# mLSTM cell and SwiGLU block on one core: the first group rebuilt, weight halves on two queues

## The chip, the core and the metric

The kernel runs on one core of a Trainium2 chip. The core has five engines with queues of their own: TensorE (PE in the profile, with its weight loads shown as PEld), VectorE (DVE, V in the code), ScalarE (ACT, A), GpSimd (POOL, G) and SyncE (SP), which here only asks for DMAs. Each engine executes its instructions in the order in which the code emits them and waits on semaphores for the others. The metric is the time of one execution on the device in microseconds; the value of a kernel is the median of its runs.

## What is computed

The first part is an mLSTM cell over q, k, v of shape (4, 8, 768, 40) with input, forget and output gates. The second part is a feed-forward block on its output, 3072 tokens of 320 features.

```python
def _attn_ref(q, k, v, i_gate, f_gate, o_gate):
    for t in range(S):
        m_new = np.maximum(f_gate[:, :, t] + m, i_gate[:, :, t])
        f_stab = np.exp(f_gate[:, :, t] + m - m_new)
        i_stab = np.exp(i_gate[:, :, t] - m_new)
        C = f_stab * C + i_stab * np.einsum('bhd,bhe->bhde', vt, kt)
        n = f_stab * n + i_stab * kt
        h_tilde = np.einsum('bhde,bhe->bhd', C, qt)
        denom = np.maximum(np.abs(nq), 1.0)
        y[:, :, t] = sigmoid(o_gate) * h_tilde / denom
...
x = y.transpose(0, 2, 1, 3).reshape(3072, 320)
g = x @ w_gate
out = (g * sigmoid(g) * (x @ w_val)) @ w_out
```

The three weight matrices are float64 in memory; q, k, v and the gates are float32.

## The kernel before

**Groups.** The 768 positions are cut into six groups of 128 (`NG`). A group holds 128 tokens of each of the four batches, so 512 tokens go through the feed-forward block together. Partitions hold the 128 positions; the free dimension holds the 32 pairs of batch and head (`BH`), split into two halves `P` of 16. Group 0 has a path of its own (the functions `first_*`), because there is no earlier state. The later groups work on blocks of 64 positions.

**Group 0.** `load` (L137) brings k, q, v into tiles whose rows are 64, 64 and 41 words per head, of which 40 are filled from memory. `first_mask`, `first_inputs`, `first_maxima` (L530 to L542) add up the exponent of the decay weights of four heads in one PSUM bank by matmuls; eight banks, keyed (u, j) with batch u and half j of its heads. `first_exp(P)` takes the exponential on ACT into `W0`. `first_turn(P, ...)` (L556) transposes k or q of two heads at a time, 128 positions wide, into `kT`, `qT`. `first_scores(P)` (L565) forms the scores in four banks and V multiplies them into `W0` (L575). `first_own(u)` (L579) multiplies `W0` with v for one batch (`first_y`), `first_x(u)` divides, `first_gate(P)` applies the output gate, `first_seam(P, ...)` (L610) transposes x into `xT`, the right-hand side of the feed-forward block. `first_values` and `first_state` make the state for the next group. `burn` issues matmuls on zeros whose result nobody reads.

**Weights.** The hidden dimension 1536 is cut into 12 blocks of 128. A block's tile has the gate half of the weights on partitions 0 to 63 and the value half on 64 to 127. `piece_load(p)` (L161) asks for piece p: pieces 0 and 1 hold one block, the next five hold two, the last three hold a third of `w_out` each. A piece is three DMAs: the gate half on SP's queue, the value half as a large and a small one, on ACT's queue for p < 5, else on SP's. The words land in a raw buffer (two of a pool in turn, or a `home`, a tile that is free at that time). `convert(j)` makes float32 of the float64 words of a block in three steps: `scale` (two ACT operations, L212 and L214), `join` (two V operations, L221 and L222) and `rounded` (an addition on V or POOL, L229).

**The hidden layer of group 0.** `hidden(0, m)` (L698) makes block m: 20 matmuls into two banks `gv_ps` (L706; with four banks of that tag, PE can run one block ahead), then `first`, a list of conversions, then SiLU on ACT (L711) and the product on V (L712). The dictionary `ahead` says which conversions stand in block m, `slots` what is emitted behind block m: the loads, decay terms, turns, weights and scores of group 1. `project_all` (L719) follows with `o_ps`, and its dictionary `after` holds more of group 1 and the loads of group 2 (`early_squares` loads k of group 2 as 32 x 32 squares). Groups 1 to 5 run `gated` (L854) and `project_seven` (L777).

**Turns and seams of 64 rows.** `turn_one` (L313) and `seam` (L468), used for group 1, work on blocks of 64 positions with two banks each.

**Order.** Everything is in the order in which it is written (`manual_schedule`): an instruction that waits holds up all that stand behind it on its engine, and a DMA request waits on the queue of the engine that issues it.

The order in which the loads are asked for:

```python
for P in range(2):
    load(k_sb, k, 0, P)
    load(q_sb, q, 0, P)
    load(v_sb, v, 0, P)
load(o_sb, o_gate, 0, 0)
```

Of the kernel before, what the change touches and what calls it, by code (L numbers as in the profile page):

```python
# [12 lines left out]
U32 = mybir.dt.uint32  # L13
# [5 lines left out]
L = 128  # L19
# [5 lines left out]
def kernel(  # L25
# [128 lines left out]
    nc.scalar.dma_start(out=flat(f_sb), in_=gate_rows(f_gate)[:, L:])  # L154
    nc.scalar.dma_start(out=flat(i_sb), in_=gate_rows(i_gate)[:, L:])
# [3 lines left out]
    PIECES = [("gv", 0, 1), ("gv", 1, 1)] + [("gv", m, 2) for m in range(2, NFC, 2)] + [("o", m, 4) for m in range(0, NFC, 4)]  # L159

    def piece_load(p, home=None):  # L161
        kind, m, n = PIECES[p]
        if kind == "gv":
# [4 lines left out]
            queues = (nc.sync,) + 2 * (nc.scalar if p < 5 else nc.sync,)  # L168
        else:
            a, d = n, DM  # L170
            src = [(slice(0, 128), slice(0, n), moe_w_out[m * 128:(m + n) * 128].rearrange("(a p) d -> p a d", p=128))]
            queues = (nc.sync,)
        if src[0][2].dtype == F32:
            for r, cs, w in src:
# [6 lines left out]
        if home is None:  # L181
            raw = conv.tile([128, 4 * NKC * 128], U32, name="raw")
        else:
            raw = home.rearrange("p a t -> p (a t)").bitcast(U32)
        raw = raw[:, 0:2 * a * d]
        for (r, cs, w), queue in zip(src, queues):
            queue.dma_start(out=raw[r].rearrange("p (a d) -> p a d", a=a)[:, cs], in_=w.bitcast(U32))
# [47 lines left out]

    for P in range(2):
        load(k_sb, k, 0, P)
        load(q_sb, q, 0, P)
        load(v_sb, v, 0, P)
    load(o_sb, o_gate, 0, 0)  # L240
# [25 lines left out]
    idb = ident[0:BH, 0:BH]  # L266
    hot = early.tile([128, H], F32)
    cold = early.tile([128, H], F32)
    for u in range(B):
        r = slice(u * BH, (u + 1) * BH)  # L270
        nc.vector.tensor_copy(hot[r], ident[r, u * BH + u * H:u * BH + (u + 1) * H])
# [23 lines left out]
    def late_sums():  # L295
        nc.vector.tensor_tensor_scan(flat(f_sb), flat(keep1), flat(f_sb), 0.0, op0=ALU.mult, op1=ALU.add)
        nc.gpsimd.memset(step1, 0.0)
        nc.gpsimd.tensor_sub(i_sb, i_sb, f_sb)
# [191 lines left out]
    def weights_mask(P):  # L490
        for i in range(2):
            w = w_sb[half(i), heads(P)]
            nc.gpsimd.affine_select(w, w, compare_op=ALU.is_ge, fill=NEG, base=0, pattern=[[0, UH], [1, SUB]],  # L493
                                    channel_multiplier=-1)

# [26 lines left out]

    def rows(u):
        return slice(u * BH, (u + 1) * BH)
# [5 lines left out]
    def first_mask(u, j):  # L530
        wps[u, j] = bank("wps", "cell" if u < 2 else "gen").rearrange("p (h t) -> p h t", t=L)
        nc.tensor.matmul(wps[u, j], lhsT=ident_b, rhs=mask_b.unsqueeze(1).to_broadcast([128, HH, L]),
                         start=True, stop=False, skip_group_check=True)

    def first_inputs(u, j):
# [572 lines left out]
```

## Time and profile before

| what | value |
|---|---|
| median of 3 runs | 512.6 us (512.21 to 513.2) |
| the profiled execution | 513.3 us, its span 511.5 us |
| instructions | 14788 |
| PE busy | 505.1 us (99%) |
| DVE busy | 332.3 us (65%) |
| POOL busy | 255.0 us (50%) |
| ACT busy | 204.8 us (40%) |
| DMA | 43.27 MB in 205497 packets, mean 85 GB/s; 193432 packets are under 512 B |

The span runs from the first to the last instruction of the profiled execution, and that execution's own time is 1.8 us longer. A line of the timeline gives start, duration, engine, source line, operation, the tiles written and read, and how many instructions it merges; in brackets stands the idle time before it and what ended it. Matmuls overlap in the array, so a busy PE is not PE at its peak. A line of a window table gives the stretch, its length, then busy time (and count) of PE, PEld, DVE, ACT and POOL, the clock that PE was granted, the share of the DMA engines and their GB/s.

### The profile page before, as it was taken

What the parts mean: (1) busy time and instruction counts of PE and PEld (TensorE: products, weight loads), DVE (VectorE), ACT (ScalarE), POOL (GpSimd) and SP (SyncE); (2) the same over time, 40 slices, a digit from 0 to 9 for tenths busy, and PEclk for the clock granted to TensorE, in tenths of its full rate; (3) what the DMA queues carried; (4) which work ended last, traced back from release to release, by engine and by line L of the source; (5) the groups of instructions that cost most, each with busy time, mean ns of one, the idle gap of its engine ahead of it and who ended that gap; (6) DMA issues with size and microseconds to landing.
All of it is one profiled execution on the core that took longest, in us unless ns stands there. A gap on an engine that the chain in (4) does not pass through costs nothing.

```text
span 511.5 us, 14788 instructions
## 1 busy us (share of the span) xinstructions
PE 505.1 (99%) x6307; PEld 428.8 (84%) x6309; DVE 332.3 (65%) x539; ACT 204.8 (40%) x394; POOL 255.0 (50%) x274
## 2 busy tenths in 40 slices
PE   8999999999999999999999999999999999999997
PEld 4964445667888899988899888899988899988896
DVE  5779767887897777687466678467658554233421
ACT  3477655448512339312339321338421340223210
POOL 1303427475879663367652457652447650166710
PEclk9999999999999999999999999999999999999999
DMA  9999999698502992501993411993101200000001
GB/s 123 174 232 238 168 194 244 148 177 119 88 1 45 143 130 39 92 3 26 156 134 42 75 21 27 156 131 43 42 3 19 37 3 27 27 1 0 1 14 38
DMA packets 205497, 43.27 MB, mean 85 GB/s; under 512 B 193432, under 2 KB 200600, under 8 KB 205432
## 3 DMA queue, kind: packets, MB, share of 16 engines
q1 hardware_dynamic: 203444, 39.49, 49.4%
q10 hardware_dynamic: 1988, 2.85, 2.4%
q8 instruction: 49, 0.80, 0.7%
q14 instruction: 16, 0.13, 0.1%
HBM read 35.68 MB, written 4.01 MB: 78 GB/s over the span
## 4 chain that ended last, share of the span: by engine, by line
PE 91%; DMA 2%; DVE 2%; issue 1%; POOL 1%; ACT 1%; SPq 0%; DVEq 0%; ACTq 0%; POOLq 0%
PE gv_x L854 26%; PE o_ps L777 23%; PE gv_y L854 21%; PE gv_ps L706 5%; PE o_ps L723 5%; DMA w_sb<-M_dram 2%; PE inter L402 2%; PE intra L411 2%; PE sp L353 2%; PE first_y L582 1%; PE add L379 1%; POOL w_sb L493 1%; PE burn L521 1%; PE tp_kq L561 1%; PE sp L571 1%
## 5 line engine op out<-in xcount | busy, mean ns | idle before, releaser
L854 PE MATMUL gv_x<-xT,wgv_sb 64*128 64x256 f32 x720 | 89.1, 377 | 0.0
L854 PEld LDWEIGHTS gv_x<-xT,wgv_sb 64*128 64x128 f32 x720 | 69.6, 187 | 7.9 <-issue 0.2
L777 PE MATMUL o_ps<-wo_sb,h_sb 128*128 128x160 f32 x480 | 67.4, 300 | 0.0
L777 PEld LDWEIGHTS o_ps<-wo_sb,h_sb 128*128 128x128 f32 x480 | 65.6, 190 | 1.7 <-issue 1.7
L902 ACT ACTIVATE h_sb<-gv_x 128x256 f32<-128x256 f32 x30 | 11.5, 383 | 117.8 <-PE gv_x L854 117.8
L706 PE MATMUL gv_ps<-xT,wgv_sb 64*128 64x512 f32 x240 | 53.7, 596 | 0.3 <-DVE wgv_sb L229 0.3
L706 PEld LDWEIGHTS gv_ps<-xT,wgv_sb 64*128 64x128 f32 x240 | 23.6, 187 | 24.4 <-issue 23.2
L854 PE MATMUL gv_y<-q_sb,wgv_sb 64*128 64x256 f32 x360 | 44.0, 377 | 0.0
L854 PE MATMUL gv_y<-xT,wgv_sb 64*128 64x256 f32 x360 | 43.9, 376 | 0.0
L854 PEld LDWEIGHTS gv_y<-q_sb,wgv_sb 64*128 64x128 f32 x360 | 34.9, 187 | 4.2 <-DVE tmp L894 0.4
L854 PEld LDWEIGHTS gv_y<-xT,wgv_sb 64*128 64x128 f32 x360 | 35.0, 187 | 3.9
L364 POOL TENSOR_TENSOR vw_sb<-v_sb,w_sb 128x656 f32<-128x656 f32 x10 | 14.6, 1467 | 41.2 <-ACT w_sb L509 40.0
L777 PE MATMUL o_ps<-wT,S 128*128 128x160 f32 x240 | 33.4, 299 | 0.0
L777 PEld LDWEIGHTS o_ps<-wT,S 128*128 128x128 f32 x240 | 32.9, 190 | 0.0
L509 ACT ACTIVATE w_sb<-w_sb,g_T 128x64 f32<-128x64 f32 x128 | 31.0, 334 | 0.0
L854 PE MATMUL gv_x<-q_sb,sw 64*128 64x256 f32 x240 | 31.0, 376 | 0.0
L875 POOL TENSOR_TENSOR h_sb<-x_sb 128x512 f32<-128x512 f32 x12 | 15.8, 1314 | 24.6 <-ACT x_sb L874 24.6
L895 POOL TENSOR_TENSOR tmp<-tmp 128x512 f32<-128x512 f32 x15 | 20.0, 1332 | 14.5 <-DVE tmp L894 14.5
L875 POOL TENSOR_TENSOR h_sb<-tmp 128x512 f32<-128x512 f32 x13 | 16.5, 1269 | 21.5 <-ACT tmp L874 21.5
L744 POOL TENSOR_TENSOR S<-h_sb 128x256 f32<-128x256 f32 x30 | 22.6, 752 | 9.2 <-DVE h_sb L875 7.3
L854 PE MATMUL gv_y<-q_sb,sw 64*128 64x256 f32 x200 | 27.0, 388 | 0.0
L723 PE MATMUL o_ps<-wo_sb,h_sb 128*128 128x320 f32 x96 | 26.9, 437 | 0.0
(221 smaller groups left out, 984.6 us busy)
## 6 DMA issues: line engine op xcount, KB each, us to landing
w_sb<-M_dram SPq DMA_DIRECT2D x10, 512.0 KB, 7.1
k_sb<-in_k_dram SPq DMA_DIRECT2D x12, 320.0 KB, 7.4
v_sb<-in_v_dram SPq DMA_DIRECT2D x12, 320.0 KB, 5.5
o_sb<-in_o_gate_dram SPq DMA_DIRECT2D x12, 320.0 KB, 6.8
raw<-in_moe_w_out_dram SPq DMA_DIRECT2D x3, 1280.0 KB, 7.5
x_sq<-k_sb SPq DMA_DIRECT2D x64, 40.0 KB, 2.0
q_sb<-in_q_dram SPq DMA_DIRECT2D x32, 64.0 KB, 3.8
out_dram<-tmp SPq DMA_DIRECT2D x24, 80.0 KB, 1.7
```

Of the source, the lines that this page charges most:

```text
L353: nc.tensor.matmul(sp[two][half(i), a, :], lhsT=kT[feats(two), P * UA + a, half(i)], rhs=qT[feats(two), P * UA + a, half(i)], start=True, ...
L364: eng.tensor_tensor(vw_sb[:, heads(P)], v_sb[:, heads(P)], w_sb[:, heads(P), last].to_broadcast([128, UH, D1]), op=ALU.mult)
L402: nc.tensor.matmul(inter[two][half(i), a, :], lhsT=qT[feats(two), P * UA + a, half(i)], rhs=state(2 * n + i)[feats(two), P * UA + a, :], s ...
L509: nc.scalar.activation(w_sb[:, h], w_sb[:, h], AF.Exp, bias=g_T[:, n, h:h + 1], scale=-1.0)
L706: nc.tensor.matmul(ps[i], lhsT=wgv_sb[half(i), m, kc, :], rhs=x[half(i), kc, :], start=(kc == 0), stop=(kc == NKC - 1))
L723: nc.tensor.matmul(ps[u], lhsT=hid(g, m)[:, ts(u, L)], rhs=wo_sb[:, m, :], start=(m == 0), stop=(m == NFC - 1))
L744: eng.tensor_tensor(S1[:, k], lo[:, second_half], hi[:, second_half], op=ALU.add)
L777: nc.tensor.matmul(node[x][:, i], lhsT=lhs(k)[:, ts(i, L)], rhs=rhs(k), start=start and k == 0 and i == 0, stop=stop and k == KH - 1, skip ...
L854: nc.tensor.matmul(ps[:, i, cols], lhsT=lhs(c)[half(i)], rhs=rhs(c)[half(i)], start=start and c == 0, stop=stop and c == n - 1, skip_group ...
L875: (nc.vector if k == KH - 1 else nc.gpsimd).tensor_tensor(h_sb[:, 2 * k + 1], uw[:, 0], uw[:, 1], op=ALU.mult)
L895: nc.gpsimd.tensor_tensor(uw[:, :, second_half], uw[:, :, second_half], uw[:, :, first_half], op=ALU.add)
L902: nc.scalar.activation(h[:, first_half], x[:, 0, first_half], AF.Silu)
```

## The change

In group 0: q and k are loaded into a dense tile (part of `h_sb`) in the order q0, k0, q1, k1, then v; V and POOL spread them into the padded tiles. The exponent's banks are keyed (P, x), half P of the pairs and batch x, so that the first half's four banks are done before the second's begin. The turns and seams are those of 64 rows. `first_own` writes its output in two halves of 64 rows. Of the burns only the first stays; a `fill` of 14 matmuls stands before the hidden layer. Gating of the first half goes to POOL.

Weights: the first six blocks are six pieces of one block; all gate halves are asked for by SP, all value halves by GpSimd, and ACT asks for none. The rest of the gates f and i (positions 128 on) are asked for by SP after the first three gate halves. Conversions and group 1's preparation are spread anew over the slots; group 1's causal mask is a V maximum with a table (`weights_cap`) in place of POOL selections. In group 2's loads the k squares go ahead of o, and in group 1 the two sigmoids move one step.

```diff
-    nc.scalar.dma_start(out=flat(f_sb), in_=gate_rows(f_gate)[:, L:])
-    nc.scalar.dma_start(out=flat(i_sb), in_=gate_rows(i_gate)[:, L:])
+    def late_gates():
+        nc.sync.dma_start(out=flat(f_sb), in_=gate_rows(f_gate)[:, L:])
+        nc.sync.dma_start(out=flat(i_sb), in_=gate_rows(i_gate)[:, L:])
...
-    PIECES = [("gv", 0, 1), ("gv", 1, 1)] + [("gv", m, 2) for m in range(2, NFC, 2)] + [("o", m, 4) for m in range(0, NFC, 4)]
+    PIECES = [("gv", m, 1) for m in range(NFC // 2)] + [("gv", m, 2) for m in range(NFC // 2, NFC, 2)] + [("o", m, 4) for m in range(0, NFC, 4)]
...
-    def piece_load(p, home=None):
+    def piece_load(p, home=None, parts=(0, 1, 2)):
...
+            if p < 6:
+                if p in (0, 4):
+                    homes["raw"] = conv.tile([128, 4 * NKC * 128], U32, name="raw")
+                base = h_sb[:, NH - NKC:].rearrange("p m t -> p (m t)").bitcast(U32) if p in (2, 3) else homes["raw"]
+                raw = base[:, ds(2 * a * d if p in (1, 3, 5) else 0, 2 * a * d)]
...
+        for x in parts:
+            if x < len(src):
+                r, cs, w = src[x]
+                eng = nc.gpsimd if x else nc.sync
+                eng.dma_start(out=raw[r].rearrange("p (a d) -> p a d", a=a)[:, cs], in_=w.bitcast(U32))
...
+    dense = h_sb[:, NH - NKC:].rearrange("p m t -> p (m t)").rearrange("p (x h d) -> p x h d", x=4, d=D)
+    def load_dense(x, a, P):
+        nc.sync.dma_start(out=dense[:, x], in_=tokens(a, 0, P))
+    def spread(eng, x, dst, P):
+        copy(eng, dst[:, heads(P), 0:D], dense[:, x])
     for P in range(2):
-        load(k_sb, k, 0, P)
-        load(q_sb, q, 0, P)
+        load_dense(2 * P, q, P)
+        load_dense(2 * P + 1, k, P)
+    for P in range(2):
         load(v_sb, v, 0, P)
-    load(o_sb, o_gate, 0, 0)
...
-        nc.gpsimd.tensor_sub(i_sb, i_sb, f_sb)
+        nc.vector.tensor_sub(i_sb, i_sb, f_sb)
...
+    def fill(name, n, thin):
+        for x in range(n):
+            i = x % 2
+            if thin:
...
+            else:
+                nc.tensor.matmul(spare_of[name, i], lhsT=junk[half(i), 0:128], rhs=junk[half(i), H * D1:], start=True,
+                                 stop=True)
...
         for h in range(H):
-            nc.tensor.matmul(first_y[u][:, h, :], lhsT=W0[:, u * H + h, :], rhs=v_sb[:, u * H + h, :], start=True, stop=True)
+            for i in range(2):
+                nc.tensor.matmul(first_y[u][half(i), h, :], lhsT=W0[:, u * H + h, half(i)], rhs=v_sb[:, u * H + h, :],
+                                 start=True, stop=True)
...
+    GATE, VALUE = (0,), (1, 2)
     burn(7)
     for f in (first_mask, first_inputs, first_maxima):
+        for x in range(B):
+            f(0, x)
+    spread(V, 0, q_sb, 0)
+    spread(G, 1, k_sb, 0)
     first_exp(0)
+    for x in range(B):
+        first_mask(1, x)
+    turn_one(0, q_sb, qT, (V, A))
+    turn_one(0, k_sb, kT, (V, V))
+    for x in range(B):
+        first_inputs(1, x)
+    for P in range(2):
+        load(o_sb, o_gate, 0, P)
+    first_ends(0)
+    spread(G, 2, q_sb, 1)
+    spread(G, 3, k_sb, 1)
+    first_scores(0)
+    for x in range(B):
+        first_maxima(1, x)
     first_exp(1)
+    for p in range(3):
+        piece_load(p, parts=GATE)
+    turn_one(1, q_sb, qT, (V, A))
     first_values(0)
+    piece_load(0, parts=VALUE)
     first_own(0)
+    turn_one(1, k_sb, kT, (A, A))
+    nc.scalar.activation(warm, warm, AF.Sigmoid)
+    first_ends(1)
+    first_values(1)
+    late_gates()
+    for p in range(3, 6):
+        piece_load(p, parts=GATE)
+    first_own(1)
     first_x(0)
     first_x(1)
     sig(0)
+    sig(1)
+    first_scores(1)
+    scale(0)
+    first_gate(0, (G, G), G)
+    for p in range(1, 6):
+        piece_load(p, parts=VALUE)
     first_own(2)
+    first_x(2)
     first_own(3)
     first_x(3)
+    seam(0, 0, (A, A, A, A))
+    first_gate(1, (V, V), A)
+    ps0 = first_state(0, "gen")
     ps1 = first_state(1, "gen")
     join(0)
     rounded(0, V)
+    seam(0, 1, (A, V, V, A))
+    fill("add", 14, False)
+    scale(1)
+    first_kept(0, ps0, V)
+    join(1)
+    first_kept(1, ps1, A)
+    rounded(1, V)
     nc.scalar.activation(warm, warm, AF.Silu)
+    convert(2, V)
...
+    ahead = {0: [], 1: [3], 2: [4], 3: [5], 4: [6], 5: [7], 6: [8], 7: [9], 8: [10], 9: [11], 10: [], 11: []}
     slots = {
+        0: [run(piece_load, 6), run(piece_load, 7, wo_sb), run(load_all, k_sb, k, 1)],
+        1: [run(late_sums)],
+        2: [run(late_maxima), run(nc.sync.dma_start, out=M_dram, in_=flat(M_sb)), run(load_all, q_sb, q, 1),
+            run(weights_load, 1), run(load_all, v_sb, v, 1)],
+        3: [run(late_decay), run(nc.scalar.activation, step1, step1, AF.Exp)],
+        4: [run(decay_rows), run(cap_table), run(piece_load, 8)],
+        5: [run(late_turns), run(decay)],
+        6: [run(turn_one, P, k_sb, kT, (A, A)) for P in range(2)] + [run(weights_cap, 0), run(weights_cap, 1), run(piece_load, 9)],
+        7: [run(weights_sub, 1, 0), run(weights_sub, 1, 1), run(weights_exp, 0), run(weights_exp, 1), run(weigh_values, G, 0),
+            run(weigh_values, G, 1)],
+        8: [run(nc.gpsimd.memset, q_sb, 0.0), run(do_scores), run(piece_load, 10), run(load_all, o_sb, o_gate, 1)],
+        9: [run(do_weigh, 0), run(do_weigh, 1), run(do_decayed, 2)],
...
+    amid = {8: [run(turn_one, P, q_sb, qT, (A, A)) for P in range(2)], 11: [run(do_intra, 0)]}
...
-        3: [run(do_divide, 1, 1), run(load_all, o_sb, o_gate, 2), run(early_squares, 0), run(weights_cap, 0)],
+        3: [run(do_divide, 1, 1), run(early_squares, 0), run(load_all, o_sb, o_gate, 2), run(weights_cap, 0)],
...
-            at["a", 0] = [run(sig, 0), run(sig, 1)] + at["a", 0]
+            at["a", 1] = [run(sig, 0), run(sig, 1)]
```

Removed lines of the first group's order and of the old slots are left out above; they stand in the code before.

## The prediction

> **What bounds the kernel now.** I read the page first, then the chain that ended last in order of time, then engine by engine the instructions of the first 90 us, then the DMA issues with their landings. By the page, TensorE (PE) is busy for 99% of the span. From the first `gv_ps` matmul at 31.92 us on, the chain is PE work almost without a break, so the time is 31.92 us of preparation plus PE work that this change does not shorten. In that later part the stage up to 125.8 us holds 93.9 us; its PE groups add up to about 91.7 (240 `gv_ps` at 0.218 from the last line below are 52.4, 96 `o_ps` at 8.81/32 are 26.4, turns, scores, sums and seams 12.9), so at most 2.2 us can be won there. The question is when `gv_ps` starts, and whether anything stalls it later. This is the end of the preparation in the chain:
>
> ```profile
> 25.28 1.73 PE first_y L582 x16
> ...
> 27.67 0.49 DVE x_sb L590
> 28.16 0.80 DVE x_sb L596 x2
> 28.96 0.33 DVE xT L144
> 29.29 0.51 DVE wgv_sb L221
> 29.82 0.82 DVE wgv_sb L222
> ...
> 30.96 0.82 DVE wgv_sb L229
> 31.79 0.14 issue
> 31.92 17.46 PE gv_ps L706 x80
> ```
>
> The last batch's output `first_y` is ready at 27.0; then VectorE (V) alone carries the end: divide (to 28.16), gate, seam copy, join (L221, L222), add (L229). The forms that the change swaps stand side by side in the trace, 128 rows in the first group and 64 rows later:
>
> ```profile
> 10.32 1.09 PE L561 MATMUL tp_kq<-ident,k_sb 128*128 128x128 f32 x8
> 59.40 0.66 PE L318 MATMUL tp_kq<-ident,k_sb 64*128 64x64 f32 x16
> 22.97 1.20 PE L582 MATMUL first_y<-v_sb,h_sb 128*128 128x41 f32 x10
> 28.04 1.13 PE L604 MATMUL add<-vw_sb,k_sb 128*64 128x41 f32 x32
> 29.33 1.25 PE L616 MATMUL tp_x<-ident,x_sb 128*128 128x128 f32 x10 [0.16 <-ACT top L212]
> 108.75 0.84 PE L476 MATMUL tp_x<-ident,x_sb 64*128 64x64 f32 x20
> ```
>
> So a 64-row turn costs 0.66 instead of 1.09 us, a seam 0.84 instead of 1.25. A batch's output with 64 output rows is 32 instructions at 1.13/32, so 1.13 us; the 16 of now take 1.88 (18.52 to 20.40).
>
> The last view is the transfers, by stretch; the last column is GB/s:
>
> ```profile
> 14.00:19.00 5.00, 4.84 (x50) 4.52 (x46) 4.86 (x10) 2.00 (x4) 1.49 (x3) 1.00 1.44 157
> 36.00:42.00 6.00, 6.00 (x32) 3.10 (x30) 4.68 (x8) 4.06 (x6) 0.00 (x0) 1.00 1.05 326
> 179.50:181.50 2.00, 2.00 (x20) 1.54 (x17) 1.47 (x3) 0.72 (x2) 1.92 (x3) 1.00 1.31 223
> 182.00:184.00 2.00, 2.00 (x17) 2.00 (x16) 0.69 (x1) 0.00 (x0) 1.95 (x3) 1.00 1.53 156
> ```
>
> At 14 to 19 us tokens land at 157 GB/s. At 179.5 `o_sb`, whose rows are dense, lands at 223; at 182 `k_sb`, 40 of every 64 words, follows (later with small `q` pieces) at 156. In the first group k0, q0, v0 and k1 land at 8.55, 10.95, 12.8 and 15.2 (issue plus time to landing): 2.4 us for a padded load, 1.85 for `v_sb` (rows of 41 words).
>
> **Transfers after the change.** f0 and i0 still land by 5.2. The two late gate loads (160 KB) leave the front. I take v's 1.85 us for a dense load, between `o_sb`'s 1.47 (327 KB at 223 GB/s) and 2.4. From 3.8 us on (the first data at 3.2 plus f0 and i0) that gives, with 0.9 for the end of each, q0 6.5, k0 8.4, q1 10.2, k1 12.1, v0 13.9, v1 15.8, o0 17.6, o1 19.5. The first gate half, behind them on SP, lands at about 21.5; block 0's value half, asked for by POOL after its first value product (13.9+1.3), lands by 22. At 2.4 a load everything is later, block 0 at about 25.4 (26.2 now, less 0.7 for the late gates).
>
> **The preparation, step by step.** Bias: now eight banks pass three rounds on PE before `first_exp` starts at 9.54. After it, four masks end at 6.0 (burn ends 4.36, the first are 0.43 apart), four inputs take half of 1.93, and the first exp comes 1.05 after the first maxima matmul as now: 8.05, four of them to 10.1. V spreads q0 from 7.3 (after its maxima product), POOL k0 from 8.4. No row shows a spread: V between 0.49 (L221, 640 words) and 0.82 (L222), POOL between 0.29 (copy of 128) and 1.29 (product of 656); I take 0.7 for both. Either end is covered, because the turn waits for two free exp banks (9.15) and the second turn for all four (10.1); without that cover the longer end costs 0.4.
> Turns: q at 9.3 to 9.95, k at 10.3 to 10.95; V copies q's half to 10.75 and both k halves, 0.65 each, to 12.4. Scores start at 12.45, against 12.52 now: up to here nothing is gained.
> Second half: PE does the scores (2.06) and the maxima; exp(1) runs 15.55 to 17.6, three microseconds later than now. Queued behind it on ACT are one q copy and two k copies, 0.6 each, to 19.3. So scores(1) start at 19.4 (now 20.32, behind the longer turns and `first_own`). V's four products come 1.27 later and take 2.48: 20.65 to 23.1 (now 24.07). The last `first_own` takes 23.2 to 24.3, where now burn and two of 1.88 end at 27.0; the removed burns and the fill of 14 thin matmuls are covered by PE's waits. Divide and gate, 1.13+0.85, end at 26.35, against 28.96.
> End: V joins (1.31) and adds (0.82) block 0, to 28.6, then copies its seam half (0.65) to 29.3: `gv_ps` at 29.45. Beside it ACT: two sigmoids to 22.3 (the table load of 1.28 follows 19.3), `scale(0)` to 24.0, four seam copies (1.7) from 25.2, pad copy to 27.2; PE: both state sums to 27.4, last seam to 28.2. ACT is 1.2 us clear, and decides only if block 0 lands after about 23.6. Gain **2.45 us** (31.92 less 29.45); with block 0 at 25.4 the ACT queue ends at 30.85 and the gain is 1.05; with dense loads at 1.47 it stays 2.45.
>
> **POOL's queue.** Ten value loads (blocks 1 to 5) stand behind the gate products on POOL, done at 23.2, and four more (pieces 6 and 7) before its add of block 3, 1.55 us, which PE needs at 29.45 + 3 x 4.37 = 42.6. So 14 issues have 17.85 us, 1.27 each. The trace has no DMA issued by POOL. Bounds: 0.19 (POOL's copy of 16 words) to 2.68 (the longest issue of a weight half on SP, behind a full queue); nearest are the unblocked issues of such halves on SP and ACT at 0.60 to 0.71. I take 0.7: ready at 33.0, eight microseconds early, cost nothing. [...]
>
> **Later.** ACT loses its weight issues (its wait of 4.8 us before the second sigmoid goes with them, off the path). The POOL mask (four of 1.6 us) becomes two V operations of 1.21, in slack. Slot 6 makes V wait for `w_sb`: behind it stand block 9's join, the product of block 7, then subtraction, exp on ACT and, behind exp, the q copies that the scores of slot 8 need. Without a late load I get scores 0.45 us late on PE. It stays so while `w_sb` lands by 62.7. It now lands at 72.3, 46 us after block 0, with 9.65 MB between (209 GB/s); after the change 8.5 MB lie between, 40.7 us: 62.2. Against the 0.45 stand 1.2 us in which PE now waits at the sums (`add`, 85.3) for V's product of the scores, whose banks it needs: scores move from slot 9 to 8, the product stays in 9, the sums in 10, so the wait goes. In group 1 about 0.5 us stands open (127.24 to 204.29 is 77.05 us, the next groups take 76.5), since k squares go ahead of o and the sigmoid moves back one step; I count half. Together a gain of **1.0**, between a loss of 0.45 and a gain of 2.2.
>
> **Sum.** The profiled execution took 513.3 us (span 511.5); less 2.45 and 1.0 it is 509.85. The three runs' median is 512.6, 0.7 lower, so **509.15**, told as 509.2. Its own range is 507.9 to 511.0.
>
> **Rivals.**
> Slower: POOL's issues. From 1.27 us an issue on, PE waits for block 3, and at 1.52 the whole gain of 3.45 is gone. At 1.7 the add ends at 23.2 + 14 x 1.7 + 1.55 = 48.55, 5.95 us late: 515.1; at 2.68 it is 19.7 late: 528.9. For it: 18 issues on an engine that also adds blocks; against it: the plain issues of 0.60 to 0.71. [...]
> Landing no faster: the change's dense rows bring nothing, tokens come at 2.4 us a load, ACT decides the end: 1.4 us less is won, 510.55. For it: the packets read are the same 160 bytes; against it 223 beside 156 GB/s.
> Late `w_sb`: if block 0 lands at 25.4 and the rate stays 209, it lands at 66.1, 3.4 us too late: 513.95. Against it: 326 GB/s when two queues run side by side.
> More gained: all 2.2 us of the later stalls vanish and dense loads at 1.47 let the turns and exps follow each other some 0.4 sooner: 507.5.
>
> **How the numbers follow.** Forecast 0.48, landing no faster 0.14, POOL 0.18, late `w_sb` 0.08, more gained 0.12. A measurement of this kernel tells about 0.2% (1 us) from no change. Faster (under 511.6) takes 0.42 of the forecast, 0.10 of the landing case and the last case: 0.64. Same: 0.06, 0.02 of the landing case and 0.03 of POOL's: 0.11. Slower: POOL's other 0.15, late `w_sb` and 0.02 of landing: 0.25. The range, 507.2 to 515.1, leaves out POOL's dearer half and a little at the bottom.
>
> **What would show it.** Right: scores at 12.4 and 19.4, `gv_ps` at 29.5 after V's chain, and no PE wait on POOL's add near 42. Wrong: ACT's seam copies or `scale(0)` last before `gv_ps` (landing), POOL issues of over 1.27 us, or V idle before the cap on `w_sb` with PE waiting at the scores.

## The result and the profile after

| | before | after |
|---|---|---|
| median of the runs, us | 512.5 | 520.7 (519.1 to 521.6, 4 runs) |
| ratio to before, 95% interval | 1 | 1.0149 [1.0122, 1.0176] |
| profiled execution, span, us | 511.5 | 518.1 |
| first `gv_ps` of block 0, us | 31.92 | 28.76 |
| group 1 starts (first `gv_x`), us | 127.2 | 133.7 |
| from there to the end of the span, us | 384.3 | 384.4 |
| mean granted clock of PE | 0.999 | 0.993 |

The change made the kernel 1.5% slower. The preparation became 3.16 us shorter; the stage behind it, in which PE makes the hidden layer and the output of group 0, became 9.7 us longer (104.9 in place of 95.2); from group 1 on nothing changed. First the preparation, in the timeline of after (start, duration, engine, line, what, how many):

```profile
15.32 0.71 PE L342 MATMUL tp_kq<-ident,q_sb 64*128 64x64 f32 x16
16.05 1.13 PE L607 MATMUL first_y<-v_sb,h_sb 128*64 128x41 f32 x32
23.73 0.84 PE L500 MATMUL tp_x<-ident,x_sb 64*128 64x64 f32 x20
```

The 64-row turns, outputs and seams cost 0.71, 1.13 and 0.84 us, as forecast. Now the chain of waits of after, from the preparation to block 10 (start, duration, what):

```profile
23.80 7.52 DMA raw<-in_moe_w_val_dram
...
33.80 0.84 DVE wgv_sb L242
...
34.78 4.58 PE gv_ps L742 x20
...
49.38 5.39 DMA M_dram<-M_sb
...
56.22 11.67 DMA w_sb<-M_dram
...
73.20 2.28 DVE w_sb L512 x2
...
76.47 1.06 ACT qT L142 x2
...
77.57 3.69 PE sp L377 x126
81.26 10.38 PE gv_ps L742 x40
```

Before, the chain ran through `gv_ps` from 31.92 to 49.38 without a break. Now block 1 waits for its value half (7.52 us under way), and the scores of group 1 wait for the row that starts with M: M is written, `w_sb` is read back and lands at 67.9, then V subtracts, ACT takes the exponential, and behind it ACT copies the turned q. What PE waited for (engine, line, releaser: us in total, times, longest):

```profile
PE sp L377 <- ACT qT L142: 4.0, 2, 3.8
PE intra L435 <- issue: 1.9, 2, 1.3
PE gv_ps L742 <- DVE wgv_sb L242: 1.5, 1, 1.5
```

And two stretches of after around the scores (stretch, length, busy time of PE, its weight loads, V, ACT, GpSimd with counts, then granted clock, DMA share, GB/s):

```profile
73.00:77.00 4.00, 0.27 (x2) 0.00 (x0) 2.47 (x3) 2.56 (x4) 1.50 (x2) 1.00 1.03 337
77.00:84.00 7.00, 6.75 (x136) 4.96 (x138) 4.58 (x6) 6.12 (x10) 5.02 (x4) 0.54 0.02 7
```

Two things are to be seen. Behind PE's wait the granted clock is at half for nearly seven microseconds: the 126 matmuls of the scores take 3.69 us, where 128 undisturbed ones take 2.02 (at 143.46), and 40 of `gv_ps` take 10.38, where 40 at full clock take 8.64 (`o_before_out`, at 71.17); that is 3.4 us on top of the wait of 4.0. And in the same seven microseconds almost nothing is transferred (share 0.02), although weights are still missing: SP stands on a request. Both come back below.

The balance up to group 1: −3.16 (preparation), +1.5 (block 1), +4.0 (scores), +3.4 (clock), +1.0 (the gap in `intra`, 1.34 in place of 0.32), −0.8 (the sums `add`, 2.08 in place of 2.84, since they no longer wait for V's product), together +5.9 of the 6.5 us that group 1 starts later. The rest is in waits of under half a microsecond.

### The profile page after: what moved, and what is told of

Same layout as the page of the kernel before. It is cut to its first block, busy times and chain, and to the rows that moved or that the text cites. A ratio compares the mean times of both kernels' runs of the same rounds, so it can differ in the third digit from the quotient of the medians.

```text
span 518.1 us, 15078 instructions
## 1 busy us (share of the span) xinstructions
PE 504.1 (97%) x6433; PEld 425.7 (82%) x6433; DVE 334.2 (65%) x543; ACT 206.8 (40%) x401; POOL 261.9 (51%) x291
## 4 chain that ended last, share of the span: by engine, by line
PE 87%; DMA 5%; DVE 4%; ACT 2%; issue 1%; POOL 1%; SPq 0%; DVEq 0%; ACTq 0%
PE gv_x L890 25%; PE o_ps L813 22%; PE gv_y L890 20%; PE o_ps L759 5%; PE gv_ps L742 4%; PE sp L377 2%; DMA w_sb<-M_dram 2%; PE inter L426 2%; PE intra L435 2%; PE add L403 1%; DMA raw<-in_moe_w_val_dram 1%; DMA M_dram<-M_sb 1%; ACT h_sb L576 1%; PE burn L539 1%; DVE w_sb L523 0%
## 5 line engine op out<-in xcount | busy, mean ns | idle before, releaser
L742 PE MATMUL gv_ps<-xT,wgv_sb 64*128 64x512 f32 x240 | 55.2, 609 | 1.9 <-DVE wgv_sb L242 1.5
L742 PEld LDWEIGHTS gv_ps<-xT,wgv_sb 64*128 64x128 f32 x240 | 24.9, 192 | 27.1 <-issue 26.0
```

The costliest lines, as they stand in the source:

```text
L742: nc.tensor.matmul(ps[i], lhsT=wgv_sb[half(i), m, kc, :], rhs=x[half(i), kc, :], start=(kc == 0), stop=(kc == NKC - 1))
```

## The experiments

All ratios are to the kernel before, run on the same chip in the same session; its median was 515.3, 512.6, 513.7 and 514.4 us in the four rounds, so times of different rounds are compared by their ratios, or by the profiles. Diffs are against the changed kernel or the one named.

| run | what | ratio [95% interval] | group 1 starts, us |
|---|---|---|---|
| `after_again` | the changed kernel | 1.0146 [1.0097, 1.0194] | 132.9 |
| `q_turn_slot7` | q turn ahead of exp | 1.0133 [1.0085, 1.0182] | 135.5 |
| `w_before_k` | M, `w_sb` ahead of k | 1.0143 [1.0079, 1.0207] | 134.0 |
| `keep_clock` | PE busy while it waits | 1.0077 [1.0047, 1.0107] | 130.9 |
| `p1_value_early` | block 1's value half early | 1.0084 [1.0054, 1.0113] | 133.2 |
| `late` | group 1 prepared a block later | 1.0106 [1.0062, 1.0149] | 131.7 |
| `late_p1` | and block 1 early | 1.0067 [1.0042, 1.0092] | 127.4 |
| `late_p1_act` | and ACT asks | 1.0278 [1.0242, 1.0314] | 140.9 |
| `late_p1mid` | `late`, block 1 asked for in between | 1.0055 [1.0025, 1.0085] | 130.4 |
| `late_p1mid_exp7` | and exp a slot up | 1.0000 [0.9969, 1.0032] | 127.1 |
| `late_p1mid_exp7_o` | and o ahead of the k squares | 1.0090 [1.0056, 1.0125] | 128.2 |
| `o_before_out` | `late_p1mid_exp7`, o ahead of an output piece | 0.9977 [0.9953, 1.0001] | 127.8 |
| `o_before_out_p8` | and the last hidden piece ahead of v | 0.9995 [0.9970, 1.0020] | 128.4 |

### First round: one suspect at a time

`q_turn_slot7` puts the q turn ahead of the wait for `w_sb`:

```diff
-    amid = {8: [run(turn_one, P, q_sb, qT, (A, A)) for P in range(2)], 11: [run(do_intra, 0)]}
+    amid = {11: [run(do_intra, 0)]}
-        7: [run(weights_sub, 1, 0), ...
+        7: [run(turn_one, P, q_sb, qT, (A, A)) for P in range(2)] + [run(weights_sub, 1, 0), ...
```

> The changed kernel with the turn of q for group 1 moved from the middle of hidden block 8 to slot 7, ahead of the subtraction and the exp, so that its four ACT copies no longer stand behind the exp that waits for w_sb. Theory (w_sb lands at 67.9 us and holds V's cap, the exp and, behind the exp on ACT, the q copies; PE then waits from 73.3 to 77.6 and runs at half clock until 84.3): the wait of 4.3 us and some 3.5 us of half clock go, less about 1 us because SiLU of block 8 still stands behind the exp: 513 to 515 us. w_sb itself still lands at about 68. Rival (the first group and the POOL queue cost the time): no more than 1 us less, about 520. Rival (w_sb's lateness moves on to the next wait on PE, the sums in slot 10): 518 or more.

A miss. Both rivals have the number; the second, that the lateness moves on, has the mechanism too, though the next wait on PE is at block 10 and not at the sums. The scores no longer wait, but the time is the same: exp now holds the scaling of block 10 on ACT, V's join of it comes late, and PE waits 4.1 us for block 10 and runs at half clock behind that (20 matmuls of `gv_ps` take 7.32 us from 84.55 on, where 20 at full clock take 4.3). Not all of it is the queue: V's join itself is slow (first steps of V for blocks 9 and 10, then GpSimd beside the second).

```profile
71.99 0.49 DVE L234 TENSOR_SCALAR wgv_sb<-top 128x640 uint32<-128x640 uint32 x1
78.98 2.89 DVE L234 TENSOR_SCALAR wgv_sb<-top 128x640 uint32<-128x640 uint32 x1 [1.80 <-ACT top L225]
77.20 2.57 POOL L388 TENSOR_TENSOR vw_sb<-v_sb,w_sb 128x656 f32<-128x656 f32 x2 [13.13 <-ACT w_sb L530]
```

The three steps of V take 2.3 us for block 9 and 5.4 for block 10; beside the latter GpSimd runs the value products, a fill with zeros and the decay products, from 77.20 to 83.72. That would be about 3 of the 4.1 us; that GpSimd's work is the cause is not separated by a run.

`w_before_k` asks for `w_sb` ahead of the tokens:

```diff
-        0: [run(piece_load, 6), run(piece_load, 7, wo_sb), run(load_all, k_sb, k, 1)],
+        0: [run(piece_load, 6), run(piece_load, 7, wo_sb)],
-            run(weights_load, 1), run(load_all, v_sb, v, 1)],
+            run(weights_load, 1), run(load_all, k_sb, k, 1), run(load_all, q_sb, q, 1), run(load_all, v_sb, v, 1)],
```

> The changed kernel with the loads of group 1 in another order on SP: the write of M and the two w_sb loads ahead of k, q and v (k was asked for in slot 0, ahead of the write of M). Theory: M is written right when V has made it (48.1) and not behind k's landing, w_sb lands at 58 to 60 in place of 67.9, V's wait before the cap goes, the wait at the scores shrinks to about 0.5 and the clock stays at 1.00: 512.5 to 514.5. k must then land by 62 for its turn in slot 6; if it lands later the gain is less by as much. Rival (DMA bandwidth as such sets the time, whatever the order): the wait only moves to k or q and the time stays above 518.

The theory has the landing right and the time wrong. `w_sb` lands at 58.3, 9.6 us sooner, V no longer waits before the cap, and PE no longer waits at the scores. But k lands some 12 us later, and PE stands 2.1 us at the k turn: what goes ahead on SP's queue is paid by what goes behind, as the rival said. The rest of the loss is two spells of half clock of 3.4 us each, one behind a wait of 0.9 us at the decay terms (57.5) and one behind a gap of 1.7 us (93.3) of the kind that the second round shows.

`keep_clock` gives PE 18 matmuls on zeros ahead of the scores:

```diff
+    def keep_clock(m, n):
+        pre[m] = [bank("gv_ps", "gen") for _ in range(2)]
+        for _ in range(n):
+            nc.tensor.matmul(pre[m][0], lhsT=junk[:, 0:128], rhs=junk, start=True, stop=True)
...
+        8: [run(nc.gpsimd.memset, q_sb, 0.0), run(keep_clock, 9, 18), run(do_scores), ...
```

> The changed kernel with 18 matmuls on zeros put on PE in front of the scores of slot 8, into the bank that block 9 then overwrites, to fill the 3.8 us in which PE waits there. Nothing waits for less. If the half clock after the wait (granted clock 0.50 from about 77.6 to 84.3) is a consequence of PE standing still, it stays at 1.00 and about 3.5 us go: 517 us. If the clock falls for another reason, the time stays at 520.7 and the 0.50 is still there.

The clock stays at 1.00 through 74 to 92 us, the wait stays, and group 1 starts 2.8 us sooner than in the changed kernel: so much the half clock behind this wait cost, beside the 4.0 us of the wait itself. This run has a spell of half clock elsewhere, 3.4 us from 37.0, behind a wait of 1.9 us at block 1. The run's ratio is 0.6 to 0.7% under those of the two runs before it on the same chip; the intervals still overlap. Part of what was won comes back as a gap of 1.51 us in group 1, at `intra` near 152 us (0.53 in the changed kernel); that gap returns below.

`p1_value_early`:

```diff
     piece_load(0, parts=VALUE)
+    piece_load(1, parts=VALUE)
...
-    for p in range(1, 6):
+    for p in range(2, 6):
```

> The changed kernel with the value half of block 1 asked for by POOL right behind that of block 0 (about 16.3 us) and not behind the gate products (23.1). The 1.5 us that PE waits for block 1 at 33.3 us goes. By the theory this brings little in the whole, as the chain M, w_sb, exp, q copies sets the scores whatever comes before: 519.5 to 520.7, with a longer wait at the scores. Rival (the time is lost in the first group and what it delays): 519.0 or less, the 1.5 us come through.

Block 1's wait goes. The ratio, 0.5 to 0.6% under those of the first two runs, is on the rival's side, which put the time 1.7 us or more under 520.7. The profiled execution shows less: the scores now wait 5.1 us, with half clock behind that (0.50 from 77 to 84 us), and PE has a gap of 1.22 us in the state sums of the preparation, released by nothing that the profile shows. The next round tells what that gap is.

### Second round: group 1's preparation a block later

```diff
-        6: [...turn k...] + [run(weights_cap, 0), run(weights_cap, 1), run(piece_load, 9)],
-        7: [run(weights_sub, 1, 0), run(weights_sub, 1, 1), run(weights_exp, 0), run(weights_exp, 1), ...weigh_values...],
-        8: [...memset..., run(do_scores), run(piece_load, 10), run(load_all, o_sb, o_gate, 1)],
-        9: [run(do_weigh, 0), run(do_weigh, 1), run(do_decayed, 2)],
+        6: [...turn k...] + [run(piece_load, 9)],
+        7: [...turn q...] + [run(weights_cap, 0), run(weights_sub, 1, 0), run(weights_cap, 1), run(weights_sub, 1, 1), ...memset...],
+        8: [run(weights_exp, 0), run(weights_exp, 1), ...weigh_values..., run(piece_load, 10)],
+        9: [run(do_scores), run(do_weigh, 0), run(do_weigh, 1), run(do_decayed, 2), run(load_all, o_sb, o_gate, 1)],
```

Prologue and queues stay as changed; the q turn is no longer inside block 8.

> The changed kernel once more, as a control on this chip. Every theory: 1.012 to 1.018 of the kernel before, scores of group 1 late by some 4 us and the granted clock at 0.50 for about 7 us behind that.

> Group 1's preparation put back one hidden block: cap and subtraction in slot 7 with the q turn, exp in 8, scores, product and decays in 9, as the kernel before has them; the prologue and the queues stay as changed. Theory (the slots were advanced past what the weight stream can feed, and the clock follows PE's idle time): w_sb still lands near 68 but is needed 4.4 us later, PE does not wait at the scores, the clock stays at 1.00; what is left is the 3.16 us won at the start, less 1.5 of block 1, less or plus 1 for the sums: ratio 0.994 to 0.999. Rival (the transfers are too slow as such): another wait takes its place, as in the two runs in which it only moved, and the ratio stays at 1.008 or above.

The control repeats: 1.0146, a wait of 4.7 us at the scores, 6.8 us of half clock. Its profile has no wait for block 1, so that term of the balance is not in every execution.

`late` goes to the rival by its number and by what it says of the waits; its reason, transfers that are too slow as such, is tested in the fourth round. PE does not wait at the scores any more, and that is the theory's half; but the ratio is 1.0106 and not under 1. It waits 2.0 us at block 1, 2.7 us at the sums of group 1 for V's product, with 3.4 us of half clock behind that, and 1.6 in `intra`. The second was not forecast: the raw half for block 10 lands only near 75.9, ACT scales it and only then does exp, the next scaling stands behind exp, V's join of that scaling, and V's product behind the join. Here too V's three steps are slow, 3.9 us beside GpSimd's products.

> As late, and block 1's value half is asked for by GpSimd right behind block 0's. Theory: another 1.5 us less than late (wait for block 1 gone), less up to 1 us because block 0's gate half shares the stream: ratio 0.992 to 0.997. Rival (transfers as such): no better than late, since what is taken early is missed later.

The ratio, 1.0067, is outside the theory's range, but the profile says why. From group 1 on 2.5 us are lost behind a gap near 149 us. Ahead of it, in the whole stretch to group 1 PE waits once, in the state sums of the preparation (timeline of PE of `late_p1`, and below it its transfers between 25.4 and 26.8 us: queue, packets, MB, share):

```profile
24.96 0.89 PE L632 MATMUL add<-vw_sb,k_sb 128*64 128x41 f32 x23
28.26 0.98 PE L632 MATMUL add<-vw_sb,k_sb 128*64 128x41 f32 x15 [2.41 <-issue]
```

```profile
q8 instruction: 1, 0.02, 6.1%
```

PE stops in the middle of a group, between two matmuls that wait for nothing that the profile shows. In that time the trace has a transfer of another kind: one packet of 16 KB on a queue of the kind "instruction". The page of after counts 50 of them, 0.82 MB, and from one to the next PE starts 255 instructions on the mean (254 in before, with 49 packets), 252 to 260 ahead of each of the last six. From these counts and from the place of the gaps the author took them for PE's own code; that is an inference, and no run tests it. These packets beside PE's gaps, from the traces:

```
kernel                 packet starts, takes   PE goes on at   gap      place
late_p1                25.41, 1.37            28.26           2.41     state sums
p1_value_early         23.84, 1.39            26.78           1.22     state sums
late_p1mid_exp7        23.98, 1.38            26.70           0.94     state sums
after                  19.90, 1.30            (not held)      none     state sums
late                   21.49, 1.40            (not held)      none     state sums
before                 96.67, 1.37            99.41           0.32     intra
after                 103.05, 1.36           105.87           1.34     intra
late                  101.45, 1.21           103.96           1.58     intra
late_p1mid            100.07, 1.15           102.67           1.41     intra
```

PE goes on 1.3 to 1.6 us after the end of the packet, each time; and the gap stands at the same matmul of the program in each kernel, behind the 23rd of the 64 sums and the 37th to 39th of 64 `intra`. In the two kernels that ask for two value halves at about 15 us the packet starts at 23.84 and 25.41; in six kernels that ask for one there, at 19.90 to 21.84. What holds it back there no run shows. In `late_p1` the gap brings 6.8 us of half clock (0.50 from 27.4 to 34.2), so that `gv_ps` starts at 32.75.

> As late_p1, but ACT asks for the value halves of the first six blocks in place of GpSimd. Theory (the GpSimd queue is not what cost the time): within 2 us of late_p1. Rival (issues on GpSimd are dear, or its queue is served worse): 2 us or more faster than late_p1.

Both wrong, in the direction against ACT: 2.1% worse than `late_p1`. ACT stands on the requests, and behind them on ACT is the copy of `kT` for the second scores: PE waits 8.4 us there. That does not say what GpSimd's queue costs by itself; it says that a place on ACT, whose copies PE needs every few microseconds, is dearer.

### Third round: what `late` left

`late_p1mid` moves block 1's request behind GpSimd's second value product (19 us):

```diff
     first_values(1)
+    piece_load(1, parts=VALUE)
```

> As late, with block 1's value half asked for by GpSimd behind its second value product (at about 19.3 us), which is later than in late_p1 (about 15) and earlier than as changed (23.1). Theory (in late_p1 the two early value halves stood ahead of PE's own code in the transfers: its 16 KB packet of instructions started at 25.41 instead of 19.90, and PE stood still for 2.41 us in the state sums until 1.5 us after that packet's end, then ran at half clock): the packet of instructions goes out near 20, no gap in the sums, gv_ps starts by 29.3 at full clock, and block 1 waits 0.5 us or less. The later wait for V's product at the sums of group 1 (2.7 us and its half clock) stays as in late: ratio 1.004 to 1.009. Rival (what is asked for early is paid whatever the moment): a gap of 1 us or more stays in the sums or at block 1, ratio as late (1.0106).

A hit on all points: packet at 21.85, no gap in the sums, `gv_ps` at 28.8, block 1 without a wait of note (0.9 us is left elsewhere in the hidden blocks), the wait at the sums still 2.6 us with its half clock (0.50 from 88 to 90 us).

`late_p1mid_exp7` moves the exponential from slot 8 to the end of slot 7, ahead of block 10's scaling:

```diff
-            run(weights_cap, 1), run(weights_sub, 1, 1), run(nc.gpsimd.memset, q_sb, 0.0)],
-        8: [run(weights_exp, 0), run(weights_exp, 1), run(weigh_values, G, 0), ...
+            run(weights_cap, 1), run(weights_sub, 1, 1), run(weights_exp, 0), run(weights_exp, 1),
+            run(nc.gpsimd.memset, q_sb, 0.0)],
+        8: [run(weigh_values, G, 0), ...
```

> As late_p1mid, and group 1's exponentials go one slot up, so that on ACT they stand ahead of the scaling of block 10, whose weight half lands only near 75.9, and not behind it. Theory (late's 2.7 us at the sums came through the in-order queues: exp behind that scaling, the next scaling behind exp, V's join behind that, V's product behind the join): the wait at the sums and the half clock behind it go, 4 us less than late_p1mid: ratio 0.996 to 1.002. Rival (the weight stream itself is late): another wait takes its place, ratio at 1.005 or above.

A hit: 1.0000. The wait at the sums of group 1 is down to 0.4 us (the instruction packet came at 23.98 this time, and cost 0.94 in the preparation: one of the five kernels that ask in between has a late packet, and both that ask at about 15 us). The move also took GpSimd's products out of the way of most of V's steps, so it does not tell the queue from that. But the rival has a part: PE now waits 2.5 us at 114 us for the last piece of the output weights, which SP asked for at 92.65; the kernel before asked at 89.80 and did not wait. And from group 1 on the profiled execution takes 388.1 us in place of 384.3: a gap of 1.5 us near 150 us, with 3.4 us of half clock behind it.

`late_p1mid_exp7_o`:

```diff
-        3: [run(do_divide, 1, 1), run(early_squares, 0), run(load_all, o_sb, o_gate, 2), run(weights_cap, 0)],
+        3: [run(do_divide, 1, 1), run(load_all, o_sb, o_gate, 2), run(early_squares, 0), run(weights_cap, 0)],
```

> As late_p1mid_exp7, and SP asks for o ahead of the 16 pieces of the k squares in group 0, as the kernel before does. Theory (putting the squares ahead of o cost group 1: o, the output and the next squares then follow later on SP, V waited 1.8 us for those squares in late_p1, and PE 1.44 us behind V): the next squares are asked for some 2.5 us sooner, the gap of 0.5 to 1.4 us near 150 us goes, 0.5 to 3 us less than late_p1mid_exp7. Rival (the order of the two loads is hidden): the same time within 0.5 us.

A miss, and a clear one: 1.0090. The gap near 150 us does shrink (1.52 to 0.47), and its cause was right: V waits for the next squares, and PE for V. But the 16 pieces of the squares before them are asked for 4.6 us later (120.05 in place of 115.46); V stands 6.1 us ahead of their turn, which ends at 134.7, PE waits 2.8 us at the start of group 1 behind it, with half clock (0.51 from 138 to 140 us). A second spell of half clock (0.50 from 118 to 120) stands behind the wait for the last output piece, which both kernels have. With the sooner stage the changed order is the better one.

### Fourth round: bytes or order

With the three waits gone the kernel was level with the one before, while its preparation ended 2.3 us sooner. `o_before_out` asks for group 1's o ahead of the second output piece:

```diff
-        8: [run(weigh_values, G, 0), run(weigh_values, G, 1), run(piece_load, 10)],
+        8: [run(weigh_values, G, 0), run(weigh_values, G, 1), run(load_all, o_sb, o_gate, 1), run(piece_load, 10)],
-        9: [..., run(do_decayed, 2), run(load_all, o_sb, o_gate, 1)],
+        9: [..., run(do_decayed, 2)],
```

> As late_p1mid_exp7, and SP asks for group 1's o (640 KB) ahead of the second piece of the output weights and not behind it. Theory (SP's order, not the bytes: SP stands on that piece for 10.9 us, until block 11 has left its buffer, and the transfers fall to a share of 0.35 between 75 and 80 us; o and all that follows on SP come 3 us later than they could, the last output piece among them, for which PE waits 2.5 us at 111): share near 1 between 70 and 77, the last output piece asked for at about 90 in place of 92.65, PE's wait for it 0.5 us or less; group 1 starts at 125.5 or earlier; ratio 0.992 to 0.999. Rival (the bytes: PE cannot run ahead of a stream that is full): the wait stays at 1.5 us or more or reappears elsewhere before group 1, ratio 0.999 or above.

SP's requests and one stretch of `late_p1mid_exp7`, then the same of `o_before_out` (start, duration, what; the stretch as above, share and GB/s at its end):

```profile
68.67 10.88 SPq L200 DMA_DIRECT2D raw<-in_moe_w_out_dram  x2
92.65 0.43 SPq L200 DMA_DIRECT2D raw<-in_moe_w_out_dram  x1
75.00:80.00 5.00, 4.62 (x140) 3.05 (x138) 4.57 (x6) 4.61 (x7) 1.83 (x3) 1.00 0.35 130
```

```profile
71.14 8.13 SPq L138 DMA_DIRECT2D o_sb<-in_o_gate_dram  x2
90.50 0.43 SPq L200 DMA_DIRECT2D raw<-in_moe_w_out_dram  x1
75.00:80.00 5.00, 5.00 (x40) 2.09 (x40) 3.13 (x4) 3.76 (x5) 4.78 (x4) 1.00 1.06 300
```

The theory of order holds in the profile. SP no longer stands 10.88 us on two output pieces, of which the second needs a buffer that block 11 still fills; the transfers between 75 and 80 us go from a share of 0.35 to 1.06, the last output piece is asked for 2.15 us sooner, and PE's wait for it is gone. The ratio, 0.9977 [0.9953, 1.0001], is the best of all and on the edge of what can be told from the kernel before; from `late_p1mid_exp7`, 1.0000 [0.9969, 1.0032], it cannot be told. Group 1 does not start by 125.5, as expected, but at 127.8: in the profiled execution block 0's gate half landed at 27.8, 3 us later than in `late_p1mid_exp7`, and PE stood 2.7 us at the last seam, behind ACT's copies, and began `gv_ps` at 32.1 at half clock (0.50 from 32 to 34 us). From there to group 1 it took 95.6 us, against 97.5 in `late_p1mid_exp7`. The larger gain stands behind it: from group 1 on it is 384.5 us in place of 388.1, with the k squares asked for 2.5 us sooner and a gap near 150 us of 0.5 us, without half clock.

> As o_before_out, and the piece of blocks 10 and 11 goes ahead of v on SP. Theory: the piece lands some 6 us sooner (near 70), block 11 leaves its buffer sooner, SP stands less; PE has no wait before group 1 that it did not have in o_before_out: within 1.5 us of it, ratio 0.990 to 0.999. Rival: v then lands too late for GpSimd's product and the state sums, PE waits 1 us or more at the sums, ratio 0.002 or more above o_before_out.

Just outside the theory's range of ratios (0.999), and nothing gained; PE has no wait at the sums, so v was not too late, and the rival is out. The same late gate half opens it (27.9).

## Why the prediction was wrong

**Right: the preparation.** The exponentials at 8.01 and 15.40 (8.05 and 15.55 forecast), scores at 12.26 and 18.98 (12.45 and 19.4), V's products at 20.25 (20.65), the gate products done at 25.8 (26.35), `gv_ps` at 28.76 (29.45). The gain there is 3.16 us, 0.7 more than forecast. The dense loads came as forecast too: k0 at 8.04, k1 at 11.63, v0 at 13.59 (8.4, 12.1, 13.9 forecast), and V's seam copy was the last step before `gv_ps`.

**Right: GpSimd's queue.** The rival with the largest weight. GpSimd's row of the preparation in after:

```profile
23.14 1.20 POOL L200 DMA_DIRECT2D raw<-in_moe_w_val_dram  x2
```

0.60 us a request (0.7 forecast, danger from 1.27), block 3's addition at 39.85, and PE never waited for it. With the waits between them the 14 requests took from 23.14 to 36.72, 0.97 us each, still under 1.27. Of the 14, the one that met V's first join step (L234, 25.70 to 26.19) took 0.86 us, the others 0.54 to 0.66; whether that step is the cause no run tests.

**Wrong: the landing of `w_sb`.** This is the step that failed: "8.5 MB lie between, 40.7 us: 62.2", against a need at 62.7. It landed at 67.9. The rate of 209 GB/s was right; two amounts were too small. Block 0's landing was put at 21.5 to 22; its gate half landed at 24.3. And between that landing and the one of `w_sb` 9.25 MB were moved and not 8.5 (the transfers of before between 26.17 and 72.30, then of after between 24.25 and 67.89):

```profile
DMA packets 17926, 9.66 MB, mean 209 GB/s; under 512 B 14371, under 2 KB 14689, under 8 KB 17921
DMA packets 17523, 9.25 MB, mean 212 GB/s; under 512 B 14558, under 2 KB 15901, under 8 KB 17517
```

Both amounts come from GpSimd's queue: the sum followed SP's order and did not count what GpSimd's requests take of the same transfers. The bytes that it lacked are, but for 0.1 MB, the value half of blocks 10 and 11 (0.66 MB). GpSimd asks for it 1.3 us behind the second `w_sb` request, and it lands at 65.4 and 66.0, ahead of `w_sb`:

```profile
57.48 0.64 POOL L200 DMA_DIRECT2D raw<-in_moe_w_val_dram  x1 [0.27 <-issue]
```

The other runs bear this out. In the ten traces of the changed kernel and its variants in which this value half is asked for within 2.4 us behind the second `w_sb` request, `w_sb` takes 11.4 to 12.0 us from there to its landing; in `late_p1`, `late_p1_act`, `w_before_k` and `o_before_out_p8`, in which it is asked for later or has already landed, 7.1 to 8.6 us. At block 0 it is the same: its value half, asked for by GpSimd at 14.97, lands at 21.3, ahead of the gate half; in `late_p1_act`, in which no value half is asked for before 21.6, the gate half lands at 21.6, as forecast.

With half a microsecond of slack both went straight into the wait. The slack was small because the change moved group 1's cap, exponential and scores one block (4.4 us) ahead, and PE came 3.16 us sooner on top. `late` undid the first part alone, and the scores did not wait.

**The late `w_sb` rival** had this chain, with a chance of 0.08 and a landing at 66.1, and priced it at 3.4 us. The wait was 4.0 us, so the place was right; that the size is near is in part luck, since the rival put block 0 later than it came (25.4) and kept the 8.5 MB. Its price lacked what follows.

**Missing: the clock.** The forecast had no term for it, since the kernel before shows full clock throughout this stage. Behind a wait of 3.8 us it was at half for 6.8 us, 3.4 us in price, and `keep_clock` shows it by itself (2.8 us). The spells of half clock are 3.4 us long in `late`, 6.8 in `late_p1` and 6.8 here. In the fifteen traces all ten of PE's idle times of 2.56 us or more, behind its start, have half clock with them; of the 22 between 0.9 and 2.5 us ten have (0.92 at 57 us in `w_before_k`, 1.44 at 149 us and 2.41 in `late_p1`) and twelve have not (2.0 at block 1 in `late`, 2.48 in `late_p1mid_exp7`). What decides between them stays open.

**Missing: block 1.** The sum timed block 3 as the first block that GpSimd's queue could hold up, by its addition. Block 1's value half was asked for behind the gate products at 23.14 and took 7.5 us to land; PE waited 1.5 us.

**Right in part: the stalls that should go.** The wait at the sums did go, but it was worth 0.8 us and not 1.2. The forecast took the wait of PE's weight loads (PEld) for one of PE; PE's matmuls wait 0.2 us there and are spread over a little more (waits of before, the sums of before, then of after):

```profile
PEld add L379 <- DVE w_sb L360: 1.2, 3, 0.8
PE add L379 <- DVE w_sb L360: 0.2, 1, 0.2
```

```profile
85.27 0.31 PE L379 MATMUL add<-vw_sb,k_sb 64*64 64x41 f32 x2
85.78 2.33 PE L379 MATMUL add<-vw_sb,k_sb 64*64 64x41 f32 x126 [0.20 <-DVE w_sb L360]
```

```profile
91.57 2.08 PE L403 MATMUL add<-vw_sb,k_sb 64*64 64x41 f32 x128
```

The half of 0.5 us from the move of the sigmoid and of the k squares did not come: group 1 onward is the same, 384.4 in place of 384.3.

**What the gain was worth.** The experiments show that a sooner start of `gv_ps` is only worth something if SP's order keeps up: with all named waits gone, 2.3 us won at the start had turned into 2.5 us at the output weights, because SP stood on a full buffer. But for `w_sb` and block 3's addition the forecast took the hidden blocks as PE work that nothing can hold up, since there was nothing to see in the profile before.

**Open.** Why block 0's gate half lands at 27.8 and 27.9 us in `o_before_out` and `o_before_out_p8`, where it decides the start of `gv_ps`, and at 23.8 to 24.7 in the three other kernels that ask for block 1's value half at about 19 us. Whether V's join is slow because of GpSimd's products. Whether the instruction packets could be brought sooner was not tried.

## What to carry to other kernels

When a change makes a stage start sooner, list for each wait behind it how much slack the kernel before had, not only whether it waited: loads that were just in time become waits, and an engine that works in order hands each of them to its neighbours (here `w_sb` came 5.2 us after its need, and through V and ACT PE waited 4.0). Count the bytes of every queue that is asked in the same time (here 0.66 MB of GpSimd's queue landed ahead of `w_sb`, which took some 3 us longer with them). Price a stall of PE by what these fifteen traces show: from 2.56 us on at least 3.4 us of half clock each time (1.7 us lost), from 0.9 us on in ten of 22 cases. Before a request that must wait for a buffer, put those that need not (`o_before_out`: the last output piece asked for 2.15 us sooner).

## What the runs showed that was not expected

- Packets of 16 KB on an instruction queue stand beside PE's gaps, and PE goes on 1.3 to 1.6 us after a packet's end (that they are PE's code is inferred). With two value halves asked for at about 15 us such a packet came 2.0 to 5.5 us later, and PE stood for up to 2.41.
- Half clock with short idle times: 0.92 us of PE's idle time had 3.4 us of it (`w_before_k`), 2.41 had 6.8 (`late_p1`). Every spell ahead of the kernel's end in the fifteen traces is 3.4 us long, or two or three times that.
- A value half on GpSimd's queue, asked for just behind `w_sb`, lands ahead of it, and `w_sb` takes 11.4 to 12.0 us in place of 7.1 to 8.6.
- V's three conversion steps of a block took 5.4 us in place of 2.3 while GpSimd ran its products (`q_turn_slot7`).
- The same requests on ACT in place of GpSimd cost 2.1%, since ACT's copies stand behind them (PE waits 8.4 us for one).
